# A gated attention and feed-forward kernel: attention steps taken out of the last unit of the first token half, another order of sums and splits, and an earlier turn of the first output tile

## The chip, the cores and the metric

The kernel runs on one core of one Trainium2 chip. The metric is the device time of one execution in microseconds (us); lower is better. Before the change it is 1744.81 us, the median of three runs (1742.91, 1745.12, 1744.81).

## The reference, cut to what matters

Two paths read the same 2048 tokens of 576 numbers (x), and a gate mixes them:

```python
g = _sigmoid((x * gate_w).sum(-1, keepdims=True))
a = _A_ref(x, A_wq, A_wk, A_wv, A_wo, A_beta)   # 32 heads of 18, four segments of 512 tokens
b = _B_ref(x, B_w_gate, B_w_up, B_w_down)       # (silu(x @ w_gate) * (x @ w_up)) @ w_down, width 4608
return g * a + (1 - g) * b
```

Inside a segment, path A is softmax attention of a token over the tokens up to it. It is mixed, head by head, with what a memory matrix M of the earlier segments returns: `o = g * a_mem + (1.0 - g) * a_dot`, where `a_mem = phi(q) M / (phi(q) z)` and M and z are summed from phi(k) and v of each segment. The result goes through wo. Everything is float32.

## The kernel before, in words

**Precision.** A float32 operand is split into a high part (a copy by ACT, the scalar engine) and a remainder (a subtraction by DVE, the vector engine): the helper `split`, lines 127 to 129, which the profile shows as L128 and L129. A product is then high x high, high x low and low x high.

**First stage (to about 223 us).** Segment by segment, s = 0 to 3, nine chains of 14 matmuls (`qk`, L346; `products`, L149) make the tiles of q and k. Then eight `v_step`s (L375) make v: each has 14 matmuls into a PSUM bank from `v_tile` (L108), which ACT and DVE empty (L385 to L391). The list of banks at L108 is used in order: the first eight numbers are those of segment 0, the next eight (and the repeats of 5, 6, 7) those of the later ones. The chains of segment 0 use banks 0 to 4 (`first_tile`), those of the later segments banks 0 to 2 (`chain_tile`). Between the v_steps of one segment the five row blocks of x for the next are split (`x_split`; the last by `xs_split`, L162 and L163).

**Second stage (223 to about 1650 us).** The feed-forward path runs in 72 units: two token halves (segments 2 and 3, then 0 and 1) of 36 feature tiles f. In a unit, seven sets of matmuls (`seven`, L993: six matmuls at L998 and one at L1001) make the gate and up products of 128 features by 1024 tokens in Strassen's way: seven products from sums of blocks, instead of eight. Their x operands `XO[j]` are blocks of x and differences of them, split; so each half needs its own set, which `x_second` (L962) makes for the second half around the break. The weight operands come from `w_make` (L248; sums on POOL, the GpSimd engine; splits on ACT and DVE at L260 and L263) or, for the first two tiles of the second half, from `w_fetch`. PSUM banks a, y and xx are passed on between the sets (L1055 to L1080); ACT reads the Silu table and then the Exp table again in every unit (L1072 and L991). The result is split into hh and hl: for f = 2, 5, 8, ... by `split` (L128, L129), for the others by `split_by` (L940, L941).

Every third unit is busy: it also does 16 groups of nine matmuls (`down_group`, L851) that multiply hh and hl of three finished tiles by w_down, and adds them to ya (L856). After the last unit of the first half there is a **break** of ten beats for the 16 groups of its last three tiles, without sets.

**What orders the work.** `manual_schedule` keeps the written order on every engine. After each set comes a `tick`, and with it a `beat` (L943). A beat runs what was deferred to it (`defer(k, fn)`: k beats on; the tables `LOADS`, `SUMS`, `PARTS`, `HIGH` and `LOW` hold such offsets, `PARTS` being the splits of x and `SUMS` the differences of its blocks), does its share of the groups, and gives `credit` to attention by `TICK[half][busy]` (L43): 1 in a busy beat, 0.57 or 0.47 in the first five beats of another unit, 0.5 in the break's last eight beats. A whole credit buys one step of `att_gen` (L794): 394 steps in all, six to a pair of heads. A step reduces a score bank (`s_bank`, L720 and L726), takes exponentials (`e_bank`, L738), makes float16 parts (`p_bank`, L752 and L753), transposes them by DMA (`x_bank`, L757), or multiplies by v (`v_unit`, L768 and L769). Nearly all DMAs are issued on SP's queue, in the written order.

When attention is done, `c_open` (L865) frees its memory and defers the third stage's loads: six chunks of wo (`wo_load`, L883: load, cast five beats on at L891, remainder seven beats on at L892) and the first two tiles of the attention result (`c_load`, L894).

**Third stage.** For 16 tiles of 128 tokens, `c_tr` (L911) adds the memory part on POOL (L913), turns the tile by five transposes (L917, L919) and splits it; `products` by wo follows, one tile later, in two halves of columns, and is mixed with the feed-forward result. The last 16 groups are spread between these steps by `downs` (L1108).

Of the kernel before, what the change touches and what calls it, by code (L numbers as in the profile page):

```python
# [27 lines left out]
FT = 36  # L28
# [11 lines left out]
XL = 5  # L40
KEPT = 2
HALF = ((2, 3), (0, 1))
TICK = ((0.57, 1.0), (0.47, 1.0))  # L43
QUIET = (5, 6, 7)
LEAD = 3
HIGH = (2, 3, 3, 7, 7, 8, 9)
# [1 line left out]
SHARE = (0, 0, 2, 2, 3, 3, 3, 3)  # L48
BREAK = 10
LOADS = ((-3, 0, 0), (-2, 0, 1), (3, 1, 0), (4, 1, 3), (4, 0, 3), (5, 0, 2), (5, 1, 1), (6, 1, 2))  # L50
SUMS = ((2, 0, 1), (9, 0, 4), (10, 1, 1), (11, 1, 4), (13, 1, 2), (14, 1, 6), (17, 0, 2), (18, 0, 6))
PARTS = ((1, 0, 0), (4, 0, 1), (10, 1, 0), (12, 1, 5), (12, 1, 3), (13, 1, 1), (14, 1, 2), (15, 1, 4), (16, 1, 6),
         (16, 0, 5), (17, 0, 3), (18, 0, 2), (19, 0, 4), (20, 0, 6))
FIRST = (9, 10, 11, 15, 16, 17, 18)
SLOT = (0, 3, 2, 1, 4, 6, 5)
RPOS = (0, 1, 4, 2, 5, 6, 3)
# [9 lines left out]
def gated_mix(ctx, tc, xT, xrest, wf, wfr, wfh, wd, wv, wo, beta, cmask, ident, bmask, out):  # L66
# [32 lines left out]
    def banks(*ids):  # L99
        turn = cycle(ids)  # L100
        return lambda shape=(P, L): ps.tile(list(shape), F32, name=f"bank{next(turn)}")
# [3 lines left out]
    pair_tile = banks(3, 4)  # L105
    first_tile = banks(0, 1, 2, 3, 4)
    lone_tile = banks(7)
    v_tile = banks(5, 6, 7, 3, 4, 5, 6, 7, *8 * (5, 6, 7))  # L108
    a_tile = banks(0)
    x_tile = banks(1)  # L110
    y_tile = banks(2)
# [15 lines left out]
    def split(hi, lo, src):  # L127
        nc.scalar.activation(hi, src, AF.Copy)  # L128
        nc.vector.tensor_sub(lo, src, f32(hi))  # L129
# [31 lines left out]
    def xs_split(xs, raw):  # L161
        nc.scalar.activation(xs, raw, AF.Copy)  # L162
        nc.vector.tensor_sub(xs[64:128], raw[64:128], f32(xs[64:128]))  # L163
# [520 lines left out]
    with ExitStack() as st:  # L684
# [176 lines left out]
        wos, tiles = [], {}  # L861
# [49 lines left out]
        def c_tr(o, me):  # L911
            if me is not None:
                nc.gpsimd.tensor_add(o[:, 0:D], o[:, 0:D], me)  # L913
            nc.gpsimd.tensor_copy(o[:, 576:640], o[:, 512:576])
            ta = half_tile([P, 4, P])
            for k in range(4):
                nc.tensor.transpose(ta[:, k], o[:, P * k:P * k + P], idt)  # L917
            tb = lone_tile([P, P])
            nc.tensor.transpose(tb, o[:, 512:640], idt)  # L919
            oh = cps[0].tile([P, 4, P], F32R, name="oh")  # L920
            ol = cps[0].tile([P, 4, P], F32R, name="ol")
            os_ = cps[0].tile([P, P], F32R, name="os")
            split(oh, ol, ta)
            xs_split(os_, tb)
            r = []
            for k in range(4):
                r += [oh[:, k], ol[:, k], oh[:, k]]
            return r + [os_, os_]
# [7 lines left out]
        credit = [-1.0]  # L936
# [6 lines left out]
        def beat(k=None, half=0):  # L943
            for fn in due.popleft() if due else ():
                fn()
            busy = 1 if groups else 0
            share = 2 if k is None else SHARE[k]
            for n in range(max(share, 1)):
                if groups and n < share:
                    down_group(*groups.pop(0))  # L950
                if n % 2 or (not busy and (n or k in QUIET)):
                    continue
                credit[0] += 0.5 if k is None else TICK[half][busy]
                if credit[0] >= 1:
                    credit[0] -= 1
                    if next(att, att) is att:
                        c_open()
# [4 lines left out]
        def x_second(new, rest):  # L962
# [3 lines left out]
            def load(z, q):  # L966
                b, kt = ((0, z), (1, z), (0, 2 + z), (1, 2 + z))[q]
                r[z, q] = wop.tile([P, L], F32, name="wo_") if z else raw_tile()[:, :L]
                nc.sync.dma_start(r[z, q], xT[HALF[1][b], :, kt])
# [6 lines left out]
            def parts(z, j):  # L976
                new[j][z] = x_slot(SLOT[j], z)
                split(new[j][z][:, 0], new[j][z][:, 1], r[z, (0, 0, 3, 2, 1, 3, 2)[j]])

            def fetch(j):  # L980
                rest[j] = xr_tile(j)
                nc.sync.dma_start(f32(rest[j]), xrd[j])

            todo += [(o, lambda z=z, q=q: load(z, q)) for o, z, q in LOADS]
            todo += [(o, lambda z=z, j=j: parts(z, j)) for o, z, j in PARTS]
            todo += [(o, lambda z=z, j=j: total(z, j)) for o, z, j in SUMS]
            todo += [(6 + j, lambda j=j: fetch(j)) for j in range(7)]
# [5 lines left out]
        def seven(t, j, first=True):  # L993
# [6 lines left out]
                    n += 1  # L1000
            nc.tensor.matmul(t, rem[:, RPOS[j]], XR[j], start=False, stop=True, skip_group_check=True)  # L1001

        draw = {}
        for o, fn in start:
            defer(o - 7, fn)
        for pos, (half, f) in enumerate(seq):
# [3 lines left out]
            nxt = seq[pos + 1] if pos + 1 < len(seq) else None  # L1010
            if q == 0 and f:
                groups += feed(half, f - 1)
            plan = []
            if nxt:
                plan += w_fetch(nxt[1]) if nxt[0] and nxt[1] < KEPT else w_make(*nxt)
                if nxt != (0, 1):
                    plan.append((1 if nxt[1] else 10, lambda f=nxt[1]: r_fetch(f)))
                for n, h in enumerate(BLOCKS.get(pos, ())):
                    plan += r_block(h, 4 * n)
                if f + 2 < FT:  # L1020
                    wraw_of[f + 2] = [None, None]
                    for u in range(2):
                        plan.append(((2, 5)[u] if f or not half else 5 + u, lambda u=u, f=f: wraw_of[f + 2].__setitem__(u, w_load(f + 2, u))))
# [84 lines left out]
        def downs(k):  # L1108
            for _ in range(min(k, len(groups))):
                down_group(*groups.pop(0))  # L1110

        ffs = {n: f_load(n) for n in range(2)}
        for n in range(17):
            if n < 16:
                if n + 2 < 16:
                    tiles[n + 2] = c_load(n + 2)
                    ffs[n + 2] = f_load(n + 2)
                nxt = c_tr(*tiles.pop(n))
                downs(2 if n else 4)
            if n:  # L1120
                tt = order[n - 1]
                ff = ffs.pop(n - 1)
                for hf in range(2):
                    c = slice(288 * hf, 288 * hf + 288)
                    t = chain_tile()
                    products(t[:, :288], ops, w_mov(wos[hf], 288))
                    downs(1)
                    if hf == 0:
                        nc.vector.tensor_scalar_mul(ff, ff, g1[:, tt:tt + 1])
                    nc.vector.scalar_tensor_tensor(ff[:, c], t[:, :288], gg[:, tt:tt + 1], ff[:, c],  # L1130
                                                   op0=OP.mult, op1=OP.add)
                    if hf == 0 and sent:
                        nc.sync.dma_start(*sent.pop(0))
                    if n == 16:
                        nc.sync.dma_start(out[0, P * tt:P * tt + P, c], ff[:, c])
                if n < 16:
                    sent.append((out[0, P * tt:P * tt + P, :], ff))
            ops = nxt
# [54 lines left out]
```

## Time and profile before

| | |
|---|---|
| median of three runs | 1744.81 us |
| profiled execution | 1747.73 us |
| its span, first to last instruction | 1746.0 us |
| granted TensorE clock, mean | 0.998 |
| HBM read, written | 165.76 MB, 76.09 MB |

The profile shows one execution. PE is TensorE's matmuls, PEld its weight loads, DVE the vector engine, ACT the scalar engine, POOL GpSimd, SP the engine that issues DMAs (SPq its queue). A row of a timeline has the start in the span, the duration, engine, line, operation, what is written and read, shapes and count; a bracket at its end tells how long the engine was idle before it, and what ended that. A row of the windows has the stretch, its length, the busy time of PE, PEld, DVE, ACT and POOL with instruction counts, the granted clock, the DMA engines' share and GB/s. A row of the chain of waits has start, duration and what was waited for.

### The profile page before, as it was taken

Reading aid. Unit: us, or ns where it says so; the run is one execution under the profiler, and the core shown is the slowest. Engines: PE = TensorE matmul, PEld = TensorE weight load, DVE = VectorE, ACT = ScalarE, POOL = GpSimd, SP = SyncE. Lnnn points to the kernel's source line nnn. Section 1 sums busy time; section 2 is a strip of 40 time slices with the busy share of each in tenths; the row PEclk is TensorE's granted clock in tenths of the full one; section 3 lists DMA queues with packets and bytes.
Section 4 is the critical chain, followed back from the end, with each engine's and each line's share of the span. In section 5 each row is a group of like instructions: output and inputs, shape, how many; then the busy total and the mean of one; then the engine's idle time right before and its main releaser. Section 6 shows DMA issues by size and latency. Waiting matters only on the chain.

```text
span 1746.0 us, 34931 instructions
## 1 busy us (share of the span) xinstructions
PE 1715.8 (98%) x11868; PEld 1483.9 (85%) x11868; DVE 1368.6 (78%) x3231; ACT 1093.6 (63%) x2198; POOL 936.3 (54%) x1194
## 2 busy tenths in 40 slices
PE   9999999999999999999999999999999999999999
PEld 7899978878888888887887788888888888888799
DVE  6567587989898889898989677787888777887655
ACT  7666575765676577667656755665666576656511
POOL 4434645656665656665666555555555555555221
PEclk9999999999999999999999999999999999999999
DMA  7654499998998888897979976777687668866544
GB/s 263 237 190 154 149 307 179 213 221 180 225 216 206 175 207 199 187 199 192 209 146 287 263 176 132 188 168 157 156 185 173 155 149 186 169 129 147 168 134 139
DMA packets 524003, 328.06 MB, mean 188 GB/s; under 512 B 411184, under 2 KB 460336, under 8 KB 523824
## 3 DMA queue, kind: packets, MB, share of 16 engines
q1 hardware_dynamic: 523824, 325.83, 76.6%
q8 instruction: 93, 1.52, 0.4%
q14 instruction: 86, 0.70, 0.1%
HBM read 165.76 MB, written 76.09 MB: 139 GB/s over the span
## 4 chain that ended last, share of the span: by engine, by line
PE 78%; ACT 8%; DVE 4%; DMA 3%; issue 3%; POOL 2%; SPq 1%; DVEq 0%; ACTq 0%; POOLq 0%
PE bank L998 29%; PE bank L851 25%; PE bank L151 10%; PE bank L1001 5%; PE bank L720 3%; PE bank L768 2%; ACT L1072 1%; PE bank L769 1%; ACT L991 1%; DMA pt<-p 1%; ACT pe L738 1%; PE bank L406 1%; POOL ws L256 1%; DVE hl L941 1%; PE bank L342 1%
## 5 line engine op out<-in xcount | busy, mean ns | idle before, releaser
L753 POOL TENSOR_TENSOR p<-pe,p 128x512 f16<-128x512 f32 x320 | 374.4, 1170 | 457.7 <-DVE p L752 438.2
L851 PE MATMUL bank<-dw,hh 128*128 128x320 f32 (+1 forms) x2304 | 491.2, 306 | 4.1 <-ACT hh L128 2.8
L851 PEld LDWEIGHTS bank<-dw,hh 128*128 128x128 f32 x2304 | 383.3, 191 | 15.6 <-ACT hh L128 3.1
L738 ACT ACTIVATE pe<-bank,mb 128x512 f32<-128x512 f32 (+3 forms) x512 | 246.2, 522 | 219.7 <-DVE mb L726 216.0
L851 PE MATMUL bank<-dw,hl 128*128 128x320 f32 (+1 forms) x1152 | 341.6, 297 | 0.2 <-DVE hl L129 0.2
L726 DVE CUSTOM_DVE_ANT_0 scr<-bank,cm 128x512 bf16<-128x512 f32 (+3 forms) x512 | 246.1, 481 | 7.4 <-PE bank L720 0.6
L851 PEld LDWEIGHTS bank<-dw,hl 128*128 128x128 f32 x1152 | 219.1, 190 | 0.4 <-DVE hl L129 0.4
L856 DVE TENSOR_TENSOR ya<-bank,ya 128x320 f32<-128x320 f32 x352 | 157.7, 452 | 78.7 <-PE bank L851 77.9
L1001 PE MATMUL bank<-xr,rh 128*128 128x512 f32 x504 | 196.3, 390 | 0.0
L746 POOL TENSOR_SCALAR_AFFINE_SELECT pe<-pe 128x256 f32<-128x256 f32 (+1 forms) x320 | 151.1, 473 | 31.2 <-ACT pe L738 21.6
L752 DVE CAST p<-pe 128x512 f16<-128x512 f32 x320 | 145.3, 454 | 2.3 <-DMA pt<-p 2.3
L256 POOL TENSOR_TENSOR ws<-raw 128x256 f32<-128x256 f32 x140 | 123.2, 880 | 15.8 <-DVE wo__22847 L263 4.1
L720 PE MATMUL bank<-kst,qst 108*128 108x512 bf16 (+3 forms) x512 | 125.4, 306 | 5.0 <-ACT pe L738 4.9
L1001 PEld LDWEIGHTS bank<-xr,rh 128*128 128x128 f32 x504 | 94.6, 188 | 20.5
L941 DVE TENSOR_TENSOR hl<-row,hh 128x512 fp32r<-128x512 f32 x120 | 101.4, 845 | 10.8 <-ACT hh L940 10.4
L1065 ACT ACTIVATE row<-bank 128x512 f32<-128x512 f32 x72 | 43.1, 598 | 93.6 <-PE bank L1001 93.5
L1070 DVE TENSOR_TENSOR row<-bank,row 128x512 f32<-128x512 f32 x72 | 49.6, 689 | 58.4 <-ACT bank L1069 58.2
L1072 ACT ACT_TABLE_LOAD x72 | 92.4, 1283 | 1.3
L991 ACT ACT_TABLE_LOAD x72 | 92.4, 1283 | 1.0
L768 PE MATMUL bank<-v,pt 128*128 128x57 bf16 x1280 | 77.0, 188 | 8.8 <-DMA pt<-p 5.7
L1055 ACT ACTIVATE bank<-bank 128x512 f32<-128x512 f32 x72 | 41.7, 579 | 67.0 <-PE bank L1001 66.9
L366 POOL TENSOR_TENSOR q<-qr,q 128x512 bf16<-128x512 f32 x36 | 44.5, 1235 | 72.7 <-ACT q L365 61.9
(2166 smaller groups left out, 4139.0 us busy)
## 6 DMA issues: line engine op xcount, KB each, us to landing
raw<-in_wf_dram SPq DMA_DIRECT2D x140, 256.0 KB
rh<-rc SPq DMA_DIRECT2D x72, 336.0 KB
dc<-dw SPq DMA_DIRECT2D x36, 576.0 KB
dw<-dc SPq DMA_DIRECT2D x36, 576.0 KB
stk<-q SPq DMA_DIRECT2D x32, 384.0 KB
draw<-in_wd_dram SPq DMA_DIRECT2D x36, 288.0 KB
rc<-rt SPq DMA_DIRECT2D x42, 224.0 KB
vd<-vps SPq DMA_DIRECT2D x8, 912.0 KB
```

The source lines that it names most:

```text
L151: nc.tensor.matmul(t, st[n], mv[n], start=(n == 0), stop=(n == 13))
L256: (nc.gpsimd.tensor_sub if sub else nc.gpsimd.tensor_add)(src[j], p(), q())
L720: nc.tensor.matmul(t[:, c:c + w], qs[:KR, pr, P * i:P * i + P], ks[:KR, pr, 0:w], start=True, stop=True)
L726: nc.vector.tensor_tensor_reduce(scr[:, :w], t[:, c:c + w], cm[:, L - w:L], -SCALE, 3.0e38, OP.add, OP.min, m[:, k:k + 1])
L738: nc.scalar.activation(pe[:, c:c + w], t[:, c:c + w], AF.Exp, bias=m[:, k:k + 1], scale=SCALE)
L746: nc.gpsimd.affine_select(d, d, pattern=pat, compare_op=OP.is_ge, fill=0.0, base=0, channel_multiplier=1)
L752: nc.vector.tensor_copy(p[:, 0], pe)
L753: nc.gpsimd.tensor_sub(p[:, 1], pe, p[:, 0])
L851: nc.tensor.matmul(t, p, q[:, cs], start=(n == 0), stop=(n == 3 * CH - 1))
L856: nc.vector.tensor_add(ya[:, i, cs], t, ya[:, i, cs])
L998: nc.tensor.matmul(t, w[:, p, z], x[z][:, q], start=first and n == 0, stop=False, skip_group_check=True)
L1001: nc.tensor.matmul(t, rem[:, RPOS[j]], XR[j], start=False, stop=True, skip_group_check=True)
```

## The change

It does five things.

1. `v_tile` gives banks 4 and 0 to the fourth and fifth v_step, where it gave 3 and 4.
2. The last unit of the first half, and the first two beats of the break, give no credit to attention; the second half gives 0.495, where it gave 0.47, in the first five beats of its units that are not busy.
3. `SUMS` and `PARTS` are reordered: a difference of x stands several beats ahead of its split, and some splits of plain blocks come earlier.
4. The first output tile is turned in the last unit, at its fourth beat, and not after it.
5. After the last unit no groups stand between the first two turned tiles and the first products; it was four and two.

```diff
-TICK = ((0.57, 1.0), (0.47, 1.0))
+TICK = ((0.57, 1.0), (0.495, 1.0))
...
-SUMS = ((2, 0, 1), (9, 0, 4), (10, 1, 1), (11, 1, 4), (13, 1, 2), (14, 1, 6), (17, 0, 2), (18, 0, 6))
-PARTS = ((1, 0, 0), (4, 0, 1), (10, 1, 0), (12, 1, 5), (12, 1, 3), (13, 1, 1), (14, 1, 2), (15, 1, 4), (16, 1, 6),
-         (16, 0, 5), (17, 0, 3), (18, 0, 2), (19, 0, 4), (20, 0, 6))
+SUMS = ((2, 0, 1), (9, 0, 4), (11, 0, 2), (12, 1, 1), (13, 1, 4), (14, 0, 6), (14, 1, 2), (16, 1, 6))
+PARTS = ((1, 0, 0), (4, 0, 1), (8, 0, 5), (9, 0, 3), (10, 1, 0), (11, 1, 5), (12, 1, 3), (13, 0, 4), (14, 0, 2),
+         (15, 1, 1), (16, 1, 4), (17, 1, 2), (18, 0, 6), (19, 1, 6))
...
-    v_tile = banks(5, 6, 7, 3, 4, 5, 6, 7, *8 * (5, 6, 7))
+    v_tile = banks(5, 6, 7, 4, 0, 5, 6, 7, *8 * (5, 6, 7))
...
-                credit[0] += 0.5 if k is None else TICK[half][busy]
+                credit[0] += 0.5 if k is None else TICK[half][busy] if (half, f) != (0, FT - 1) else 0
...
+        early = []
...
+            if not nxt:
+                plan.append((3, lambda: early.append(c_tr(*tiles.pop(0)))))
...
-                nxt = c_tr(*tiles.pop(n))
-                downs(2 if n else 4)
+                nxt = c_tr(*tiles.pop(n)) if n else early.pop()
+                downs(2 if n > 1 else 0)
```

An entry (o, z, j) of `SUMS` or `PARTS` concerns column block z of operand j; its beat is o + 9 counted from the start of unit (0,34), so that o = 8 is the first beat of the break and o = 18 the first of unit (1,0).

## Prediction

> **What bounds the kernel now.** I read the page first, then TensorE's timeline for its idle stretches, then the queues of the other engines around each of them.
>
> ```profile
> PE 1715.8 (98%) x11868; PEld 1483.9 (85%) x11868; DVE 1368.6 (78%) x3231; ACT 1093.6 (63%) x2198; POOL 936.3 (54%) x1194
> PE 78%; ACT 8%; DVE 4%; DMA 3%; issue 3%; POOL 2%; SPq 1%; DVEq 0%; ACTq 0%; POOLq 0%
> ```
>
> TensorE is the bound: it is busy for 98% of the span, and the change removes no matmul. So the change can only win or lose where TensorE waits, or runs at a lower clock. These are its waits at the places that the change touches (the bracket is the idle time ahead of the row and what ended it), and then the clock in three stretches (the third figure from the right).
>
> ```profile
> 43.72 1.85 PE L151 MATMUL bank<-vw,xo 128*128 128x288 f32 x12 [1.26 <-DVE ph L368]
> 928.26 1.66 PE L998 MATMUL bank<-xo,wo__12856 128*128 128x512 f32 x6 [1.09 <-DVE bank L1062]
> 936.85 0.20 PE L768 MATMUL bank<-v,pt 128*128 128x57 bf16 x1 [2.21 <-DMA pt<-p]
> 943.80 0.51 PE L851 MATMUL bank<-dw,hh 128*128 128x256 f32 x2 [1.02 <-DVE ya L856]
> 1119.37 0.38 PE L720 MATMUL bank<-kst,qst 108*128 108x128 bf16 x2 [0.59 <-ACT pe L738]
> 1179.56 0.38 PE L720 MATMUL bank<-kst,qst 108*128 108x128 bf16 x2 [0.33 <-ACT pe L738]
> 1357.81 0.38 PE L720 MATMUL bank<-kst,qst 108*128 108x256 bf16 x2 [0.74 <-ACT pe L738]
> 1418.42 0.38 PE L720 MATMUL bank<-kst,qst 108*128 108x128 bf16 x2 [0.93 <-ACT pe L738]
> 1597.05 0.19 PE L768 MATMUL bank<-v,pt 128*128 128x57 bf16 x1 [1.21 <-ACT pe L738]
> 1653.94 0.56 PE L851 MATMUL bank<-dw,hh 128*128 128x320 f32 x2 [2.80 <-ACT hh L128]
> ```
>
> ```profile
> 815.70:819.20 3.50, 3.42 (x52) 3.12 (x52) 3.37 (x10) 2.37 (x7) 3.05 (x4) 1.00 0.60 153
> 937.10:941.50 4.40, 4.40 (x28) 4.40 (x24) 4.09 (x9) 3.66 (x9) 3.23 (x4) 0.62 1.04 402
> 1654.00:1658.00 4.00, 3.58 (x15) 3.02 (x16) 3.50 (x7) 1.05 (x3) 1.65 (x2) 0.61 0.61 226
> ```
>
> A wait of 2 us costs more than itself: after the waits of 2.21 and 2.80 us the granted clock fell, which cost up to 0.38 x 4.40 = 1.7 and 0.39 x 4.00 = 1.6 us. So the losses in reach are 1.3 us in segment zero, 1.09 + 2.21 + 1.02 + 1.7 = 6.0 between the halves, 3.8 in five busy units of half 1, and 2.8 + 1.6 = 4.4 at the tail.
>
> **Banks of segment one.** v_step 3 of segment 0 moves from bank 3, which the last q/k chain still holds, to bank 4. The wait of 1.26 us goes. What is late next?
>
> ```profile
> 49.76 0.46 ACT L391 ACTIVATE vps<-r 128x288 bf16<-128x288 f32 x1 [0.92 <-DVE r L386]
> 55.17 0.82 DVE L163 TENSOR_TENSOR xs<-xo,xs 64x512 fp32r<-64x512 f32 x1 [0.60 <-ACT xs L162]
> 56.04 0.50 PE L151 MATMUL bank<-xs,qhi 128*128 128x512 f32 x1
> ```
>
> During the v_steps ACT and DVE pass the work to each other (ACT waits for DVE, DVE for ACT), with TensorE well ahead of both. Their last split of x for segment 1 ends at 55.17 + 0.82 = 55.99, and the matmul that reads it starts at 56.04: TensorE is waiting there already. Coming 1.26 us earlier, it waits that much longer. I take 0.1 us gained; the bounds are 0 and 1.3.
>
> **Between the halves.** Counting the credits of the diff by hand: unit (0,35) loses its three attention steps, the break loses two of six, and half 1 gets the five back. I follow DVE up to L1062, then ACT up to the first half of hh, for which the 16 groups of the break wait.
>
> ```profile
> 921.73 1.52 PE L998 MATMUL bank<-xo,wo__12799 128*128 128x512 f32 x6
> 923.32 0.39 PE L720 MATMUL bank<-kst,qst 108*128 108x512 bf16 x1
> 925.16 0.39 PE L720 MATMUL bank<-kst,qst 108*128 108x128 bf16 x2
> 925.97 0.68 DVE L941 TENSOR_TENSOR hl<-row,hh 128x512 fp32r<-128x512 f32 x1
> 927.51 0.69 DVE L1062 TENSOR_TENSOR bank<-bank,row 128x512 f32<-128x512 f32 x1
> 930.24 0.58 ACT L1069 ACTIVATE bank<-bank 128x512 f32<-128x512 f32 x1 [1.43 <-PE bank L1001]
> 930.73 0.62 ACT L128 ACTIVATE xo<-raw 128x512 fp32r<-128x512 f32 x1
> 931.83 0.83 ACT L738 ACTIVATE pe<-bank,mb 128x128 f32<-128x128 f32 x2
> 932.67 1.28 ACT L1072 ACT_TABLE_LOAD   x1
> 935.10 1.28 ACT L991 ACT_TABLE_LOAD   x1
> 936.50 0.61 ACT L128 ACTIVATE hh<-row 128x512 fp32r<-128x512 f32 x1
> ```
>
> Seven matmuls take 923.32 - 921.73 = 1.59 us, and a score bank adds 925.16 - 923.32 - 1.59 = 0.25. Without attention, L1062 follows the hl row directly, at 926.6 instead of 927.51, and ends at 927.2. TensorE has its third set ready at 926.5, so it waits 0.7 us instead of 1.09 and starts the fourth set at 927.25 instead of 928.26; three sets later, at 932.0, the unit ends. L1069 comes 1.98 us after the start of that set, as before: 929.2. From L1069 to the end of hh were 936.50 + 0.61 - 930.24 = 6.9 us; the exponentials go (0.8), but the split (0,5) now stands ahead of hh in ACT's queue (0.5, as from 930.73 to the next row), so 6.6 us: hh is there at 935.8. The two table loads, 2.6 us, are untouched. TensorE does six matmuls of the first group on the two earlier units (0.9 us) and waits from 932.9 to 935.8, **2.9 us**, where before attention filled part of that time; then 0.3 us for hl. This wait lies between those that dropped the clock (2.21, 2.80) and beyond, while after 1.88 us idle, ahead of the stretch at 815.70, the clock stayed at 1.00; but it may be cut by whatever window the gate counts in, so I take 0.7 of 1.7 us. After: 0.7 + 2.9 + 0.3 + 1.2 = 5.1 us, against 6.0. **Gain 0.9 us.** Bounds: nothing (2.9 us plus the whole clock loss, and the 1.02 us bank wait stays) to 3 us (no clock loss, hh 1 us earlier). The five displaced steps are the same matmuls elsewhere; sums and splits of x are the same number, and the eight sums fall on a POOL that has less attention to do, so I price the reordering at nothing; its cover is that operands of (1,0) are read 1.6 us apart.
>
> [...]
>
> One queue is passed: the operand fetches of unit (1,0) on SP each wait for the split that frees their buffer. The last now waits for split (1,6), which stands behind the second set of (1,0) on ACT, some 1.9 us later than it was issued.
>
> ```profile
> 963.41 0.66 SPq L705 DMA_DIRECT2D wo__13416<-wc  x1
> 971.26 1.52 PE L998 MATMUL bank<-xo,wo__13416 128*128 128x512 f32 x6
> ```
>
> Held behind it on SP are the rh fetch, the fetches of (1,1) and the transposes of p. It has 971.26 - 963.41 = 7.9 us, less 1.9; the slowest transfer of this stretch (the transpose that ended the 2.21 us wait) took about 6. I take 0, with a bound of 0.5 us lost.
>
> **Phase in half 1.** The five waits of half 1 stand at the second tick of a busy unit, and whether they come depends on which of the six attention steps falls there and how close the last step came before. Before, the first step of the eleven busy units is number 5, 3, 2, 1, 0, 4, 3, 2, 0, 5, 4; after, by the credits, 0, 5, 4, 3, 2, 1, 0, 5, 4, 3, 2. Giving each new unit the wait of the old one with its step and the same distance: 0, 0, 0, 0.7, 0.6, 0.2, 0, 0, 1.2, 0.9, 0.9 = 4.5 against 3.8. **Loss 0.7 us**, bounds a gain of 3.8 and a loss of 3.
>
> **Tail.** c_open moves by the credits from the second tick of (1,34) to the first of (1,35), seven ticks later, and brings wo's six chunks (c0 to c5: load, cast on ACT, remainder on DVE) with it. The first tile is turned inside (1,35): five transposes and its splits, beside slack.
>
> ```profile
> 1641.24 1.46 SPq L888 DMA_DIRECT2D raw<-in_wo_dram  x2
> 1644.47 0.61 ACT L891 ACTIVATE wo<-raw 128x480 fp32r<-128x480 f32 x1 [0.78 <-DMA raw<-in_wo_dram]
> 1649.32 0.39 PE L1001 MATMUL bank<-xr,rh 128*128 128x512 f32 x1
> 1650.22 1.28 ACT L991 ACT_TABLE_LOAD   x1
> 1652.49 0.66 DVE L892 TENSOR_TENSOR wo<-raw,wo 128x480 fp32r<-128x480 f32 x1 [1.02 <-ACT wo L891]
> 1663.19 0.30 PE L151 MATMUL bank<-wo,oh 128*128 128x288 f32 x1
> ```
>
> ```profile
> 1660.95 2.40 PE bank L851 x18
> 1663.35 1.86 PE bank L151 x14
> ```
>
> Before, TensorE ends the last set at 1649.6, waits for hh, and by 1663.2 has turned two tiles and done six groups. After, it turns the second tile and wants the products of the first, which need c0, c1 and c2 split. ACT is free about 0.7 us earlier than now (no cast delays L1069), at 1650.9, and then does c0, c1, hh, c2 at 0.5 us each, to 1653. DVE does the two products of the gate, then c0, hl, c1, hl, c2 at 0.65 us each, to about **1654.8**: TensorE stands idle for some 4 us there, and the clock drops as it does now. Twelve matmuls at half clock end at 1657.6; a group and the second products (1.9 us), a second group (groups are 1.2 us) and the third tile's transposes (0.5) end at 1662.7. It has then done three tiles' transposes, two groups and two products, 7.5 us, against two tiles' and six groups, 8.1: level with before at 1663.2. c4 is loaded once c0's remainder frees its buffer (1652.0) and lands 3.2 us later (1641.24 to 1644.47), c5 1.7 us behind it; split at 1658.2, just before the second products want them. **Change 0**, bounds a gain of 4.4 us and a loss of 4.
>
> **Sum.** -0.1 - 0.9 + 0.7 + 0 = -0.3 us. The profiled execution took 1747.73 us, 1.7 around its span of 1746.0; it would take 1747.4. It stands 2.9 above the median of 1744.81, so I forecast **1744.5 us**, no change within 0.2% (3.5 us, about what a measurement of this kernel can tell from no change).
>
> **Rivals.**
> (a) Faster, 1739.5 us, chance 0.27: the waits go as the diff lays them out. Between the halves the remaining wait does not drop the clock (1.2 better), the tail's two pieces of idle time are too short to drop it either (1.6), wo's chunks are split a microsecond or two earlier than I count (1.5), the phase is neutral (0.7): 5 us below. For it: the clock held after 1.88 us. Against it: hh and c2 stand behind counted rows.
> (b) Slower, 1749 us, chance 0.16: SP stands at c4's load until DVE has c0's remainder, and behind it are ff and the third and fourth tiles. If the third tile (about 3 us of queue, then a POOL addition) lands after 1662.7, TensorE waits there again, some 3 us with the clock, and the fourth tile follows late: 4.5 us. It decides from about 1 us more than I count.
> (c) The bank edit does what it says, and its 1.26 us survive: 1743.3, inside the forecast (chance 0.1 of the 0.57 for the forecast).
>
> The forecast's own range is 1741.3 to 1748.3; with most of (a) and part of (b) the range is 1739 to 1749.5. Chances: faster 0.27, within 0.2% 0.57, slower 0.16.
>
> **What would show it.** The first chain of segment 1 still waits for xs at 56. Between the halves: no 2.21 us wait for pt, one of about 3 us on hh instead, with or without a clock of 0.6 behind it. Tail: TensorE's first long wait is for wo, not for hh. Wrong would be: a tail whose products start by 1652, a break without a wait on hh, or a wait for o at the third tile.

## The result and the profile after

The changed kernel takes **1751.14 us** (median of six runs, 1749.1 to 1752.6), the kernel before 1744.33 beside it (six runs, 1742.3 to 1745.69): a ratio of 1.0035, 95% interval 1.0025 to 1.0045. It is 4.4 to 7.9 us slower, outside the range on record. The profiled execution took 1751.22 us, span 1749.5, mean granted clock 0.996.

The page of the changed kernel has the same picture as before: TensorE is busy for 98%, and a little more of the chain lies on ACT.

```profile
PE 1717.8 (98%) x11868; PEld 1485.1 (85%) x11868; DVE 1367.4 (78%) x3231; ACT 1094.6 (63%) x2198; POOL 937.1 (54%) x1194
PE 78%; ACT 10%; DVE 4%; DMA 3%; issue 3%; POOL 2%; SPq 0%; DVEq 0%; ACTq 0%; POOLq 0%
```

TensorE's timeline of the changed kernel has these waits at the places of the prediction (idle time and its releaser in the bracket). Numbers of lines below L1003 are one to three higher than before.

```profile
924.57 1.66 PE L998 MATMUL bank<-xo,wo__12856 128*128 128x512 f32 x6 [0.61 <-DVE bank L1065]
933.28 0.55 PE L851 MATMUL bank<-dw,hh 128*128 128x320 f32 x2 [2.78 <-ACT hh L128]
968.85 1.61 PE L998 MATMUL bank<-xo,wo__13384 128*128 128x512 f32 x6 [1.32 <-DMA wo__13384<-wc]
993.46 1.66 PE L998 MATMUL bank<-xo,wo__13632 128*128 128x512 f32 x6 [1.51 <-ACT bank L1072]
1653.84 0.66 PE L917 MATMUL bank<-idt,o 128*128 128x128 f32 x4 [1.51 <-POOL o L913]
1655.82 0.61 PE L151 MATMUL bank<-wo,oh 128*128 128x288 f32 x1 [1.01 <-ACT wo L891]
1657.79 0.85 PE L151 MATMUL bank<-wo,oh 128*128 128x288 f32 x2 [1.12 <-DVE wo L892]
```

Between the halves the waits came as forecast (0.61 and 2.78 us). New are 1.32 us in the second unit of the second half and 1.51 in its third, where there was none.

The windows show where the time went. From the start of (0,35) each kernel is cut into four: (0,35) with the break; (1,0) to (1,2); (1,3) to (1,34); and the rest. Before:

```profile
920.14:960.13 39.99, 35.66 (x247) 31.62 (x246) 36.81 (x76) 23.59 (x44) 24.84 (x24) 0.96 1.07 289
960.13:996.39 36.26, 36.26 (x199) 28.80 (x198) 23.43 (x59) 27.32 (x52) 17.49 (x23) 1.00 1.07 288
996.39:1637.71 641.32, 637.52 (x4577) 550.15 (x4576) 504.36 (x1232) 400.67 (x805) 347.63 (x445) 1.00 0.72 160
1637.71:1746.00 108.29, 101.50 (x722) 97.73 (x720) 61.27 (x117) 26.39 (x58) 22.70 (x29) 0.98 0.47 154
```

And the changed kernel:

```profile
917.38:954.82 37.44, 33.80 (x201) 30.13 (x200) 31.65 (x61) 21.29 (x39) 18.75 (x18) 0.95 0.81 227
954.82:995.18 40.36, 37.53 (x237) 29.56 (x236) 22.70 (x54) 26.85 (x50) 17.31 (x22) 1.00 1.06 298
995.18:1640.45 645.27, 639.09 (x4585) 550.77 (x4584) 509.52 (x1249) 403.77 (x810) 354.77 (x453) 1.00 0.73 162
1640.45:1749.50 109.05, 101.96 (x722) 98.60 (x720) 61.03 (x120) 26.27 (x59) 22.92 (x28) 0.97 0.45 150
```

The changes are -2.55, +4.10, +3.95 and +0.76, together +6.3 us. (The spans differ by only 3.5, because the profiled execution of before took longer up to (0,35): it got there at 920.14, and all later kernels but e11 at 914.8 to 917.5.) The break is shorter, but 1.86 us of that is work of TensorE that now runs behind it (busy time 35.66 before, 33.80 after), and the units after it give back more.

### The profile page after: what moved, and what is told of

The parts are those of the page before. It is cut to its first block, busy times and chain, and to the rows that moved or that the text cites. A ratio compares the mean times of both kernels' runs of the same rounds, so it can differ in the third digit from the quotient of the medians.

```text
span 1749.5 us, 34918 instructions
## 1 busy us (share of the span) xinstructions
PE 1717.8 (98%) x11868; PEld 1485.1 (85%) x11868; DVE 1367.4 (78%) x3231; ACT 1094.6 (63%) x2198; POOL 937.1 (54%) x1194
## 3 DMA queue, kind: packets, MB, share of 16 engines
q8 instruction: 93, 1.52, 0.4%
## 4 chain that ended last, share of the span: by engine, by line
PE 78%; ACT 10%; DVE 4%; DMA 3%; issue 3%; POOL 2%; SPq 0%; DVEq 0%; ACTq 0%; POOLq 0%
PE bank L998 29%; PE bank L851 25%; PE bank L151 10%; PE bank L1001 5%; PE bank L720 4%; PE bank L768 2%; ACT L1075 2%; PE bank L769 1%; ACT L991 1%; ACT pe L738 1%; DMA pt<-p 1%; PE bank L406 1%; ACT row L1075 1%; POOL ws L256 1%; PE bank L452 1%
## 5 line engine op out<-in xcount | busy, mean ns | idle before, releaser
L151 PE MATMUL bank<-xo,qhi 128*128 128x512 f32 x264 | 83.2, 396 | 0.4 <-ACT vps L391 0.4
```

The source lines that it names most:

```text
L151: nc.tensor.matmul(t, st[n], mv[n], start=(n == 0), stop=(n == 13))
```

## The experiments

Each was timed in five rounds beside the kernel before; ratios are to it. The table has the lengths of the four stretches in us, from the unit starts in each trace.

| kernel | ratio (95% interval) | (0,35), break | (1,0) to (1,2) | (1,3) to (1,34) | rest |
|---|---|---|---|---|---|
| before | 1 | 39.99 | 36.26 | 641.32 | 108.29 |
| changed | 1.0035 (1.0025 to 1.0045) | 37.44 | 40.36 | 645.27 | 109.05 |
| e1 banks | 0.9992 (0.9984 to 1.0001) | 41.43 | 36.25 | 641.35 | 107.37 |
| e2 sums | 1.0024 (1.0014 to 1.0033) | 42.52 | 38.08 | 641.31 | 109.50 |
| e3 turn | 0.9980 (0.9971 to 0.9989) | 40.00 | 36.25 | 641.31 | 104.42 |
| e4 banks, sums, turn | 0.9998 (0.9989 to 1.0007) | 43.53 | 38.24 | 641.31 | 104.54 |
| e5 credit | 1.0025 (1.0016 to 1.0033) | 36.23 | 36.99 | 645.27 | 112.77 |
| e6 changed, 0.51 | 0.9989 (0.9980 to 0.9998) | 38.13 | 39.82 | 642.97 | 103.56 |
| e8 sums, two put back | 1.0021 (1.0012 to 1.0030) | 43.58 | 37.15 | 641.35 | 106.94 |
| e9 sums, block 1 only | 1.0007 (0.9998 to 1.0015) | 39.96 | 37.19 | 641.31 | 106.82 |
| e9 sums, block 0 only | 1.0003 (0.9995 to 1.0012) | 42.72 | 36.13 | 641.26 | 107.10 |
| e10 credit 0.51, turn | 0.9963 (0.9951 to 0.9976) | 36.67 | 37.28 | 642.89 | 104.29 |
| e11 as e10, 0.6, start -3 | 1.0076 (1.0062 to 1.0090) | 37.85 | 40.28 | 640.90 | 108.23 |
| e12 as e10, 0.6 | 0.9988 (0.9979 to 0.9996) | 35.15 | 38.78 | 643.55 | 107.53 |
| e13 changed, old sums | 1.0009 (1.0000 to 1.0017) | 36.18 | 36.99 | 645.30 | 109.08 |
| e14 changed, stores later | 1.0036 (1.0023 to 1.0048) | 37.37 | 40.89 | 645.27 | 109.29 |
| e15 sums, stores later | 1.0018 (1.0008 to 1.0027) | 42.52 | 37.38 | 641.50 | 109.01 |

My theory after the result was that the credit edit carries the loss: displaced attention fills SP's queue in (1,0) to (1,2) and shifts the phase of the rest. The rivals were the reordered sums, the early turn, and the clock.

**The parts alone.** First the banks:

```diff
-    v_tile = banks(5, 6, 7, 3, 4, 5, 6, 7, *8 * (5, 6, 7))
+    v_tile = banks(5, 6, 7, 4, 0, 5, 6, 7, *8 * (5, 6, 7))
```

> Only the list of banks of v_tile is changed (banks 4 and 0 for the fourth and fifth v_step). In the trace of the changed kernel the first unit started 2.2 us earlier than in the one of before, and the eleventh 4.4 us earlier. Theory 1 (that lead is the spread between two executions, and the bank edit is worth about nothing, since the split xs sets the first chain of segment 1): within 1 us of before, 1743.3 to 1745. Rival (the bank edit gives these 2 to 4 us): 2 to 4.4 us faster, 1740 to 1742.

It took 1743.87 us: no difference that can be told from none. The first matmul on xs of segment 1 starts at 52.9 to 53.9 us in five traces with the edit (the changed kernel, e1, e4, e6, e13) and at 52.6 to 53.8 in seven without it (e2, e3, e5, e8, e10, e11, e12); only the execution of before had 56.04. In those seven the wait that the edit removes was 0 to 0.66 us, not 1.26. The edit is worth nothing that these runs can tell (interval -1.4 to +0.2 us), and the lead of the first stage was the spread between executions.

Then `SUMS` and `PARTS` alone (the diff is that of the change):

> Only SUMS and PARTS are reordered. Theory 1 (the loss comes from the attention steps moved from the break into the second half, not from the order of the sums): the stalls between the halves stay with pt (2.2 us, with its half clock), the second half's first three units take what they take before, and the time is within 1 us of before. Rival 2 (the new order itself makes the operands of the second half's first sets late: the fetch of w_down or of the wo__ buffers stands behind x's transfers): units (1,0) to (1,2) lose 3 to 4 us and the time is 3 to 4 us above before. The first stage of this kernel is that of before word for word, so it also shows how far two executions of the same first stage lie apart: theory 1 expects (0,0) to start within 2 us of 221, the rival of the banks at 223.

It took 1749.97 us, 4.2 above before by the ratio. **My theory fell here**: the reordering by itself costs as much as the credit edit. SP's timeline shows where. First e1, whose sums are those of before:

```profile
943.83 1.43 SPq L757 DMA_TRANSPOSE pt<-p  x1
945.37 0.53 SPq L705 DMA_DIRECT2D wo__13271<-wc  x1
953.06 5.45 SPq L1036 DMA_DIRECT2D ffd<-ya  x8
958.61 0.64 SPq L705 DMA_DIRECT2D wo__13416<-wc  x1
```

The same places with the reordered sums, 1.2 us later as a whole, and then, from the timelines of POOL and TensorE of the same kernel, the sum and the wait that belong to them:

```profile
945.75 1.43 SPq L757 DMA_TRANSPOSE pt<-p  x1
954.10 0.35 SPq L705 DMA_DIRECT2D wo__13278<-wc  x1
960.76 5.73 SPq L1036 DMA_DIRECT2D ffd<-ya  x8
966.61 0.64 SPq L705 DMA_DIRECT2D wo__13419<-wc  x1
```

```profile
952.32 1.75 POOL L974 TENSOR_TENSOR wo__12968<-wo__12968,wo__12954 128x512 f32<-128x512 f32 x1
...
971.74 1.61 PE L998 MATMUL bank<-xo,wo__13419 128*128 128x512 f32 x6 [1.57 <-ACT row L1074]
```

The fourth operand of the second half is fetched into the buffer of a block of x. It comes free when the last sum and the last split have read that block. Before, that is at 945.3; now it is when POOL's sum ends, at 952.32 + 1.75 = 954.07, and SP issues the fetch at 954.10. From 947.18 to 954.10 SP stands (its queue issues nothing until that fetch may go), and behind it stand eight stores of ffd and the operands of the last sets of (1,0). The row's releaser names ACT, whose result came 0.04 us ahead of the matmul; the operand wo__13419 landed only 0.14 us ahead of it, at 971.60, so it was late as well.

The changed kernel without its credit edit (banks, sums and turn):

> The changed kernel with TICK and the credit line as before (banks, order of sums and early turn stay). Theory 1 (the credit edit carries the loss: minus 2.6 us at the break, plus 4.1 us in the first three units of the second half, plus 4 us in its busy units, together plus 5.5): this kernel is 5 to 6 us faster than the changed one, 1743 to 1746, with c_open in unit (1,34) and so no wait for wo in the third stage. Rival 2 (the reordered sums carry the loss): 1748 to 1750. Rival 3 (the early turn and the missing groups carry it): 1748 to 1751, with TensorE waiting for wo or for the turned tile after the last set.

It took 1745.27 us, as theory 1 says, but for another reason: the sums' loss (4.2, e2) and the turn's gain (3.5, e3 below) nearly cancel. The credit edit alone:

```diff
-                credit[0] += 0.5 if k is None else TICK[half][busy]
+                credit[0] += 0.5 if k is None else TICK[half][busy] if (half, f) != (0, FT - 1) else 0
```

(with 0.495 in place of 0.47)

> Only the credit edit: no attention in (0,35) and the break's first two beats, and 0.495 in the second half. Theory 1: 5 to 6 us above before, 1749.5 to 1750.5; (1,1) waits for the fetched wo__ buffers, the waits of the busy units of the second half add up to about 6 us against 3.8. Rival 2 (sums and splits): within 1 us of before. Rival 4 (the clock: the loss is one more window at half clock, 1.5 to 1.7 us each, in an execution): the number of half-clock windows goes with the time and the credit edit alone gives plus 1.5 us at most.

It took 1749.6 us, as forecast, but only in part for the reasons forecast. The waits of the busy units add up to 6.1 us, as theory 1 says; but no unit waits for a fetched operand, and (1,0) to (1,2) take only 0.7 us more, without a wait of TensorE over 0.15 us, so that this is the displaced work itself. Over the second stage the edit is nearly even: 3.8 us less at the break, 4.7 more behind it. The loss is after the last set, where the rest takes 112.77 us in place of 108.29. There ACT, DVE and TensorE of this kernel show

```profile
1654.75 0.60 ACT L891 ACTIVATE wo<-raw 128x480 fp32r<-128x480 f32 x1 [1.43 <-DMA raw<-in_wo_dram]
1657.00 0.82 DVE L856 TENSOR_TENSOR ya<-bank,ya 128x320 f32<-128x320 f32 x2
1657.55 0.90 PE L851 MATMUL bank<-dw,hh 128*128 128x320 f32 x2 [5.79 <-DVE ya L856]
```

The last chunks of wo come late; their remainders stand on DVE ahead of the additions to ya, and TensorE has no bank for its next group for 5.79 us.

The early turn alone:

```diff
+            if not nxt:
+                plan.append((3, lambda: early.append(c_tr(*tiles.pop(0)))))
...
-                nxt = c_tr(*tiles.pop(n))
-                downs(2 if n else 4)
+                nxt = c_tr(*tiles.pop(n)) if n else early.pop()
+                downs(2 if n > 1 else 0)
```

> Only the early turn: the first output tile is turned in the last unit, and the groups between the first turned tiles and the first products are taken out. Credits, banks and sums as before. The change with its credits left as before (banks, sums and turn) gained 3.8 us after the last set, against before's profile. Theory 1 (the turn gains what the late wo takes away again): 3 to 4.5 us faster than before, 1740 to 1742, no half-clock window after the last set. Rival 3 (the turn itself costs, because the groups no longer cover the waits for wo): 0 to 3 us slower.

It took 1741.13 us, 3.5 faster, as theory 1 says: the rest takes 104.42 us, no wait of TensorE in it is longer than 0.28, and the clock there stays at 1.00. Rival 3 is out.

**The late load of wo.** One number of the changed kernel:

```diff
-TICK = ((0.57, 1.0), (0.495, 1.0))
+TICK = ((0.57, 1.0), (0.51, 1.0))
```

> The changed kernel with 0.51 in the place of 0.495. By the credits attention then ends, and wo is loaded, at the second beat of (1,34), as before the change, and not at the first of (1,35). Theory 1 (with 0.495 the late load of wo costs 4 to 4.5 us after the last set): 3.5 to 5 us faster than the changed kernel, 1745.5 to 1747.5; the waits in the busy units of the second half come in another order, plus or minus 1.5. Rival (the loss is in the second half and not in the load of wo): within 1.5 us of the changed kernel, 1749 to 1751.

It took 1742.58 us: from 6.1 us above before to 1.9 below, more than I expected. Its windows from (1,3) on:

```profile
995.47:1638.44 642.97, 638.52 (x4585) 550.43 (x4584) 511.78 (x1250) 402.16 (x809) 353.38 (x453) 1.00 0.73 163
1638.44:1742.00 103.56, 99.78 (x722) 96.48 (x720) 62.32 (x117) 26.07 (x58) 23.05 (x29) 1.00 0.49 161
```

After the last set 5.5 us are gained, and 2.3 in the units before. So with 0.495 the load of wo comes seven ticks too late, and this takes back all that the early turn gives. Credit edit with 0.51 and early turn, with the old sums and banks:

> The change without the reordered sums and without the bank edit, and with 0.51 in the place of 0.495: credit edit and early turn. Theory 1 (the break gains 3.8 us and the second half pays 4 to 5 for the displaced steps; with wo loaded as early as before the turn gains 3 to 4.5): 1740.5 to 1743, that is no better than the early turn alone. Rival (taking attention from the break is a gain by itself once wo is early): 1738 to 1740.

It took **1737.86 us**, ratio 0.9963, the fastest kernel of all: the rival's number. With wo early, attention taken out of the break is a gain of its own, about 3 us on top of the turn.

**The sums.** In the kernel of e2, two entries go back:

```diff
-SUMS = (..., (13, 1, 4), (14, 0, 6), (14, 1, 2), (16, 1, 6))
+SUMS = (..., (13, 1, 4), (13, 1, 2), (14, 0, 6), (16, 1, 6))
...
-PARTS = (..., (12, 1, 3), (13, 0, 4), (14, 0, 2), (15, 1, 1), ...
+PARTS = (..., (12, 1, 3), (13, 1, 1), (13, 0, 4), (14, 0, 2), ...
```

> The kernel with only the sums reordered (1750 us), with two entries put back: the sum (1,2) and the split (1,1) stand at 13 again and not at 14 and 15. These two are the last readers of a buffer into which the fourth operand of the second half is fetched. Theory 1 (SP stands at that fetch for 7 us until POOL's sum has read the buffer, and the 8 stores of ffd and the operands of the fifth and sixth sets of (1,0) stand behind it): the fetch is issued 5 to 8 us earlier, the fifth set of (1,0) does not wait, and the time is 3 to 4.5 us below that of the reordered sums, 1745.5 to 1747. Rival (the cost lies in the splits of the plain blocks, which now stand ahead of hl on DVE, and in a second half-clock window of the break): 1748.5 to 1750.5, no wait for an operand all the same.

It took 1747.81 us, ratio 1.0021. The fetch is issued at 948.61 (4.3 us earlier, counted from the start of (0,35)), but the next one then stands to 955.19 for its own buffer, and the stores still begin at 960.00. (1,0) to (1,2) gain 0.9 us; most of the loss stays. The time lies between the two forecasts, and TensorE still waits 0.76 us for an operand, which neither expected: freeing one buffer does not free the queue.

Then the two column blocks apart:

```diff
-SUMS = ((2, 0, 1), (9, 0, 4), (10, 1, 1), (11, 1, 4), (13, 1, 2), (14, 1, 6), (17, 0, 2), (18, 0, 6))
+SUMS = ((2, 0, 1), (9, 0, 4), (12, 1, 1), (13, 1, 4), (14, 1, 2), (16, 1, 6), (17, 0, 2), (18, 0, 6))
```

> Before, with only the entries of column block 1 of SUMS and PARTS as in the change; those of block 0 stay. Block 1's operands are in the wo__ buffers into which the fetches of the second half go. Theory 1 (two separate losses of the reordered sums: SP's stand at the fetch, from block 1, and DVE's splits of plain blocks ahead of ya in the break, from block 0): SP's stand stays (the fourth fetch is issued at about 952 to 955 in place of 945 to 946), (1,0) to (1,2) together take 37.5 to 38.2 us in place of 36.3, the break 40 to 41.5, and the time is 1.5 to 2.5 us above before, 1746.5 to 1747.5. Rival (block 1 carries all of it): 1748.5 to 1750.

> Before, with only the entries of column block 0 of SUMS and PARTS as in the change. Theory 1: no stand of SP at the fourth fetch, (1,0) to (1,2) take 36.3 us as before; two splits of plain blocks more stand ahead of hl and ya on DVE in the break, which takes 42 to 43.5 us in place of 40 to 41.4: 1.5 to 2.5 us above before, 1746.5 to 1747.5. Rival (block 1 carries all of it): within 0.8 us of before, 1744.2 to 1745.7.

(with `PARTS` likewise; the second has block 0 as in the change). 1745.35 and 1744.57 us: each alone costs little, 1.2 and 0.5 us by the ratios, with intervals that take in 0. Block 0 fits the rival, block 1 neither, and both together cost more (4.2) than the two apart. In the profiles the stretches lie where theory 1 puts them: block 1 alone lengthens (1,0) to (1,2) by 0.9 us, block 0 alone takes 42.72 us at the break against 40.0 to 41.4 in the three kernels with the old sums and the old credits (before, e1, e3). But the second does not show in its median (interval -0.9 to +2.1 us). The clock accounts for most of it: in the break of block 0 alone, and of e2, e4, e8 and e15 (42.5 to 43.6 us), the traces have 6.83 us at half clock, in that of before, e1, e3 and block 1 alone (40.0 to 41.4) 3.41. In unit (0,30) 3.41 us at half clock cost some 1.5 us, and whether they come there changes from one execution to the next (last section). Why the blocks do not add up stays open.

To see whether the stores in SP's queue matter, I issued them six ticks later, in the kernel of e2 and in the changed one:

```diff
-                if k == 0:
+                if k == 6:
                     while stores:
```

> The kernel with only the sums reordered (1750 us), with the eight stores moved in the same way. Theory 1: (1,0) takes 12.6 to 12.8 us again in place of 14.4, 1.5 to 2 us faster, 1747.8 to 1748.5; what is left of the loss is in the break. Rival (all of the loss is SP's queue): 1745 to 1746.5. Rival (none of it is): 1749.2 to 1750.5.

> The changed kernel with the eight stores of ffd issued after the seventh set of (1,0) and not after the first. Theory 1 (the fetches for the second half's first units are late because they stand behind the stores on SP): the fetch on which (1,1) waited 1.3 us is issued some 5 us earlier and the wait is gone, and with it part of the wait of 1.5 us in (1,2): 1.3 to 2.8 us faster than the changed kernel, 1748 to 1749.8. Rival (DVE and ACT make the operands late in the break): within 0.8 us of the changed kernel.

On e2 it went as theory 1 says: 1748.2 us, and (1,0) takes 12.59 us in place of 14.43; 0.9 of the gain goes again in (1,1), where TensorE waits for another fetched operand. In the changed kernel it brought nothing (1750.92 us), which is the rival's number, though the wait that is left in (1,1) is again one for a fetch. That for wo__13384 is gone, and the stores now stand ahead of other operands of (1,1):

```profile
975.32 1.61 PE L998 MATMUL bank<-xo,wo__13431 128*128 128x512 f32 x6 [1.30 <-DMA wo__13431<-wc]
```

As far as these two runs show, to move something within SP's queue there mostly chooses which set waits. Last, the changed kernel with the old `SUMS` and `PARTS`:

> The changed kernel with SUMS and PARTS as before. Theory 1 (the reordering costs 4 to 5 us in the whole change as well: 1.2 in the break, 3.4 in (1,0) to (1,2)): 4 to 5 us faster than the changed kernel, 1746 to 1747.2, with no wait for wo__ in (1,1). Rival (it costs only without the credit edit): 1750 to 1751.

It took 1745.48 us, 4.5 less by the ratios, as theory 1 says. Its first two windows, against 37.44 and 40.36 above:

```profile
915.15:951.33 36.18, 33.29 (x201) 29.95 (x200) 29.76 (x60) 20.89 (x38) 17.29 (x16) 0.95 0.94 277
951.33:988.32 36.99, 36.99 (x237) 29.72 (x236) 25.21 (x55) 27.89 (x52) 19.03 (x23) 1.00 1.03 283
```

So in the whole change the reordering costs 1.3 us at the break and 3.4 in the three units after it. On SP of this kernel:

```profile
943.50 1.29 SPq L757 DMA_TRANSPOSE pt<-p  x1
944.90 0.52 SPq L705 DMA_DIRECT2D wo__13209<-wc  x1
945.52 0.38 SPq L705 DMA_DIRECT2D wo__13237<-wc  x1
945.96 6.83 SPq L1039 DMA_DIRECT2D ffd<-ya  x8
956.27 0.78 SPq L705 DMA_DIRECT2D wo__13384<-wc  x1
```

and on SP, then on DVE, of the changed kernel:

```profile
943.26 1.24 SPq L757 DMA_TRANSPOSE pt<-p  x1
949.29 0.34 SPq L705 DMA_DIRECT2D wo__13168<-wc  x1
951.78 1.03 SPq L705 DMA_DIRECT2D wo__13214<-wc  x1
953.90 0.34 SPq L705 DMA_DIRECT2D wo__13241<-wc  x1
954.29 5.85 SPq L1039 DMA_DIRECT2D ffd<-ya  x8
963.97 0.53 SPq L705 DMA_DIRECT2D wo__13384<-wc  x1
```

```profile
947.70 1.52 DVE L129 TENSOR_TENSOR xo<-wo__12919,xo 128x512 fp32r<-128x512 f32 x1
951.02 0.73 DVE L129 TENSOR_TENSOR xo<-wo__12953,xo 128x512 fp32r<-128x512 f32 x1
952.73 1.10 DVE L129 TENSOR_TENSOR xo<-wo__12933,xo 128x512 fp32r<-128x512 f32 x1
```

Each of the three fetches is issued within 0.1 us of the end of one of these splits (949.22, 951.75, 953.83), and each of the splits was moved one to three beats back. For the first SP stands 4.8 us, for the second 0.1, for the third 1.1. The stores begin at 954.29 in place of 945.96, which is 6.1 us later when both are counted from the start of (0,35).

The 3.4 us are the wait of 1.32 for wo__13384, which is fetched behind them, the wait of 1.51 in (1,2), and 0.5 more busy time. The wait of 1.51 goes back to SP's queue too: ahead of L1072 ACT stands 1.34 and 1.77 us for sums of weights, and POOL, which makes them, stands 5.37 us for a load of weights:

```profile
988.52 1.03 POOL L256 TENSOR_TENSOR ws<-raw 128x256 f32<-128x256 f32 x1 [5.37 <-DMA raw<-in_wf_dram]
```

In e13 POOL stands 2.08 us at this place; counted from the start of (1,0), SP issued the load 25.1 us on there, and 29.9 in the changed kernel. That the reordering costs this is shown by e2 and e13. That it costs it through SP's queue is read from these rows; no run keeps the new order and takes the fetches off the queue.

**The phase.** In half 1 the waits of the busy units were the same to 0.02 us wherever the credits were the same (3.8 us in sum with 0.47, 6.15 with 0.495, 4.44 with 0.51). So I tried credits that give every busy unit the same first step (against e10):

```diff
-TICK = ((0.57, 1.0), (0.51, 1.0))
+TICK = ((0.57, 1.0), (0.6, 1.0))
...
-        credit = [-1.0]
+        credit = [-3.0]
```

> The kernel with credit edit and early turn (1737.9 us), with 0.6 in the place of 0.51 and a start credit of -3 in the place of -1. Three steps then fall into every unit that is not busy, twelve into a busy one, so that by the credits every busy unit of the second half begins with step 0 of its pair. In all kernels so far a busy unit that began with step 0 or 5 waited 0 to 0.3 us (only 0 at step 0), and one that began with step 1 to 4 mostly 0.6 to 1.2. Theory 1 (the step at which a busy unit begins sets its wait): all eleven waits are gone, 4.4 us less from (1,3) on, with 1 us either way from the first half, whose steps shift too: 1732.5 to 1735.5. Rival (the waits come from how many steps stand ahead of the busy unit, and not from which): the waits stay between 3 and 6 us, 1737 to 1740.

> The same with a start credit of -1: every busy unit of the second half begins with step 2, which so far waited 0.59 or 0.93 us. Theory 1: eleven waits, 6.5 to 10 us in all in place of 4.4 with 0.51: 2 to 5.5 us above the kernel with 0.51, 1740 to 1743.5. Rival (how many steps, not which): the same as with -3, within 1.5 us.

They took 1758.19 and 1741.63 us. With step 0 all eleven waits are gone, as theory 1 says; but with step 2 they are gone too, all but one of 0.93 us, where theory 1 expected 6.5 to 10. (In both, the last exponentials of attention run in (1,30), so the last of the eleven units, (1,33), says nothing.) **Which step stands first does not set the wait by itself**; with three steps in every unit that is not busy there is next to none, which is the rival's cause, though it expected the waits of e11 to stay. What decides stays open. The time of e12 is that of theory 1, but by other waits, those of the last two units. The 16.6 us between the two arise elsewhere: the start credit shifts the steps of the first half too, and there (0,6) to (0,29) take 499.54 us with -3 and 483.38 with -1. With 0.6 both also wait 2.8 to 3.9 us in each of the last two units, which I did not follow up.

## Why the prediction was wrong

**Banks: right.** Worth nothing, since xs sets the first chain of segment 1. The 1.26 us themselves were particular to one execution.

**Between the halves: right in sum, in part by luck.** The wait on hh came as forecast, 2.78 us against 2.9, the one on L1065 with 0.61 against 0.7, the one on hl with 0.25 against 0.3, and the clock fell once. The idle time of TensorE became 0.7 us shorter (4.33 to 3.64), against 0.9 forecast; the other 1.86 us of the 2.55 are matmuls that moved. But the reordering, priced at nothing, took 1.3 us of the break's gain (e13 against the changed kernel), so without it the forecast would have been too small.

**The operand fetches: the step that failed.** "I take 0, with a bound of 0.5 us lost." I followed only the last of the fetches, the one that waits for split (1,6). The three before it wait for splits that moved as well, by one to three beats, and they stand ahead of the eight stores. The price was 3.4 us in (1,0) to (1,2) and 1.3 at the break, measured by e13. "I price the reordering at nothing; its cover is that operands of (1,0) are read 1.6 us apart" looked at when an operand is written, not at when a buffer is given back. The displaced steps add the smaller part, 0.7 us in (1,0) to (1,2) by themselves (e5), and that is their matmuls and no wait.

**Phase: right in sign, too small.** Forecast 0.7 us, measured 6.16 - 3.80 = 2.4, inside its bounds. Unit for unit, 0, 0, 0, 0.7, 0.6, 0.2, 0, 0, 1.2, 0.9, 0.9 was forecast and 0, 0, 0.72, 0.74, 0.59, 0.59, 0, 0.29, 1.22, 1.08, 0.93 came. The pattern held, but the analogy of first step and distance missed three units (by 0.7, 0.4 and 0.3 us), and e12 shows that it is not the cause.

**Tail: right in sum, and wrong in its first wait.** Forecast 0, measured +0.8 in the pair of profiles: 4.5 us lost to the late wo (e5) and 3.8 gained by the turn (e3, 104.42 against 108.29). TensorE's first long wait was not for wo but for the second tile: its memory part, me, stands on SP behind the loads of the third and fourth chunks, which wait for their buffers, so that POOL's sum is late and TensorE waits 1.51 us. SP's timeline of the changed kernel:

```profile
1642.90 5.16 SPq L888 DMA_DIRECT2D raw<-in_wo_dram  x2
1648.10 0.62 SPq L897 DMA_DIRECT2D o<-atd  x1
1648.78 0.42 SPq L901 DMA_DIRECT2D me<-med  x1
```

This wait does not need the late wo: in e4, with wo as early as before, TensorE waits 1.52 us for the second tile, whose sum starts 6 us after the issue of me (4.6 in e3, where it does not wait). Together the three waits were 3.6 us, where I gave about 4. Rival (b), a third tile that is late, did not come; the loss that it names is of the size that came, from another place.

**Sum.** Forecast -0.1 - 0.9 + 0.7 + 0 = -0.3; in the terms of the table +6.3. The displaced matmuls nearly cancel in it: -1.86 at the break, +0.7 in (1,0) to (1,2) and +1.6 behind (3.95 less the 2.36 that the waits of the busy units grew), together +0.4. Of the 6.6 us between forecast and table, the fetches are 3.4, the phase 1.7, the tail 0.8, these matmuls 0.4, the break 0.2 and the banks 0.1.

## What to carry to other kernels

When operations are reordered, ask for each not only when its result is needed but when it gives back the buffer that it reads, and which queue stands for that buffer; then count everything behind the standing instruction, and follow every such fetch, not only the last. A change of several parts can hide a gain of its own: here one part gained 3.5 us alone, and with the credits at 0.51 two of them gained 6.5, while the whole lost 6. A wait that is seen in one execution only, as the 1.26 us were, is not yet a wait of the kernel.

## What the runs showed of the hardware

**Where the clock fell.** In unit (0,30) TensorE waits 1.86 to 1.91 us in 16 of the 17 profiles; the bracket names the same exponential in 12 of them and the fetch of rh in four. In seven, before among them, the clock stays at 1.00 and the unit takes 36.9 to 37.0 us; in nine it falls to half, and the unit takes 38.4 to 38.5 (36.94 in before, 38.43 in the changed kernel). The wait in the timeline of the changed kernel, the window behind it, and the wait before:

```profile
811.56 0.19 PE L768 MATMUL bank<-v,pt 128*128 128x57 bf16 x1 [1.89 <-ACT pe L738]
```

```profile
812.00:815.50 3.50, 3.50 (x36) 3.02 (x32) 2.43 (x7) 1.86 (x5) 3.50 (x4) 0.51 0.57 143
```

```profile
815.78 0.19 PE L768 MATMUL bank<-v,pt 128*128 128x57 bf16 x1 [1.88 <-ACT pe L738]
```

The prediction took 1.88 us as a length that keeps the clock. Over all 17 profiles it is close to an even chance, worth 1.5 us from run to run. The clock records of before and of the changed kernel show more. But for 0.96 and 0.82 us behind the last instruction, the stretches at half clock are 3.413 us long or, once, twice that: in before at 938.12 and 1654.91, in the changed kernel at 812.04, 934.92 and 1655.13 (6.827 us). In each of the two executions they start whole multiples of 3.413 us apart: 210 times in before, 36 and 211 times in the changed kernel. So I counted TensorE's idle time in steps of 3.413 us from these starts, in each execution by itself. In the step ahead of a fall TensorE was idle for 2.15 and 2.60 us in before, and for 1.89, 2.03 and 1.83 in the changed kernel. Among the other steps at full clock, from 70 us on, the most was 1.34 us in before and 1.32 in the changed kernel. The 1.34 are the wait of (0,30): in before it lies across two steps, in the changed kernel in one. In the nine profiles that fell there, 1.76 to 1.91 us of this wait lie in one step; in six of the seven that held, 1.34 to 1.68; the seventh, e13, held with 1.85, so that the idle time of the step does not decide alone.

**Splits on DVE beside sums on POOL.** In the changed kernel a split remainder of 128x512 takes 0.68 us on DVE, and took 1.52 at 947.70 (above), while POOL's L974 ran from 947.38 to 948.68:

```profile
945.32 0.68 DVE L129 TENSOR_TENSOR xo<-raw,xo 128x512 fp32r<-128x512 f32 x1
947.38 1.30 POOL L974 TENSOR_TENSOR wo__12933<-wo__12933,wo__12919 128x512 f32<-128x512 f32 x1
```

It ended 0.54 us after POOL did, and so did the one at 952.73, which took 1.10 beside a sum that ended at 953.29. Where DVE was first (942.68, 0.68 us), it was POOL's sum that took longer, 1.75 us from 942.75 on in place of 1.3. In these three pairs the later of the two looks to have waited, and not to have run slower; that is read from their ends and shown by no run of its own. The splits at 947.70 and 952.73 are two of the three for whose buffers SP stands in the break: they took 0.84 and 0.42 us more than 0.68. I did not measure by itself what this costs.
